# Attention plus routed MLP on one core: out-projection one block later, router search two blocks later, last key tiles moved forward

## Chip, cores and metric

The kernel runs on one core of a Trainium2 chip. The metric is the device time of one execution in microseconds. The engines named below are TensorE (PE, with its weight loads PEld), VectorE (DVE), ScalarE (ACT), GpSimd (POOL) and SyncE (SP), which issues nearly all DMAs.

## What is computed

The input x is one sequence of 2048 rows of 448 numbers. A layer norm, attention with 16 heads of 28 numbers over one shared key and one shared value head, an out-projection and a residual give h. A second layer norm of h feeds a router that picks 8 rows, and only those rows go through a gated MLP:

```python
x = A_x
h = x + _A_ref(_layernorm(x), A_wq, A_wk, A_wv, A_wo)
# _A_ref: q of 16 heads, one k, one v; softmax(q k^T * 28**-0.5) v; then @ wo
xn = _layernorm(h)
# _B_ref(xn): r = xn @ w_r; idx = the 8 largest r;
#   y = silu(xn[idx] @ w_gate) * (xn[idx] @ w_up) @ w_down * sigmoid(r[idx])
#   returns xn with y added at the rows idx
h2 = h + _B_ref(xn, B_w_r, B_w_gate, B_w_up, B_w_down)
```

All tensors are bf16. The result has 2048 x 448 numbers.

## The kernel before

**Blocks.** Attention is done in 16 blocks b = 4*qb + g: 512 query rows (qb) by 4 heads (g). A block runs over 16 key tiles of 128 keys. For a key tile, PE makes the scores of the 4 heads in two units of two PSUM banks (`qk`), an engine turns them into exponentials, and PE multiplies these with the values into the block's accumulator bank 6 or 7 (`act_pv`, `dve_pv`). Exponentials are made in two ways. On most tiles ACT makes them (line 753, one ACTIVATE of 128x1024 for a unit, PSUM banks 0 to 3 in turn); this text calls one such instruction "an exponential". On a few tiles of each block DVE approximates them: four TENSOR_SCALARs of 128x512 from PSUM banks 4 and 5 (line 766) and three shifts of 128x2048 (line 772) for a tile, which this text calls Y and shift. The list `groups` and the table `where` say which tiles of a block are DVE's: none in block 0, three in blocks 4, 8 and 12, four in the others, 57 in all. That leaves 199 tiles, or 398 exponentials, to ACT.

**The end of a block** (`post_block`). DVE copies the accumulator to `Ot` (line 551). Its row of softmax sums then goes through memory: SP stores it (`l_scr<-Ot`), loads it as 128x16 (`Lc<-l_scr`), DVE takes the reciprocal (line 560), SP stores that (`l_scr<-Lc`) and loads it broadcast over partitions (`Rb<-l_scr`). POOL multiplies `Ot` and `Rb` into `On` (line 563).

**Out-projection and second layer norm** (`out_proj`). When the four heads of a query block have their `On`, four steps k of 128 rows follow. PE multiplies `On` with `wo_pad` into one PSUM bank; DVE adds the residual into `hbuf` (line 579), takes the statistics (lines 581 and 582), POOL raises the variance to the power -0.5 (line 585, tile `st`), and DVE writes the normed row, the output row and the router's score (lines 587 to 601). This text calls these DVE instructions one LN chain. After k = 3, SP stores `out_dram<-x_sb` and `xn_scr<-xn`, 448 KB each. This happens for the first three query blocks; the last one has its own shorter path (`last_pre`, `last_proj`).

**Router.** After the third query block, `first_top` gathers 1536 scores: a matmul and a copy to `r12` (line 622) and three DMAs that lay them out in one row (`xnT<-r`); the second and third wait until the first has landed. `first_max` finds the 8 largest with MAX (line 628) and their places with MAX_INDEX (line 630), both on DVE. `second_top` uses the places to gather 8 rows by two indirect DMAs on POOL's queue. After the last block the remaining 512 scores are searched and the MLP of the 8 rows runs: the tail of the program.

**What sets the order.** The program's five instruction streams are made by `_Graph`. Each step is entered with a priority, its due time in key tiles: block b starts at 16*b. `plan` lists the steps with a duration and a latency for each (the number `lat` for a DMA, 2000 ns unless given), takes at each point the available step with the lowest priority, and so fixes the order on every engine. On the chip each engine runs its list strictly in that order, and waits on semaphores where data comes from another engine. `at(t, f, ...)` near line 803 gives out-projection, router and the rest their due times. `misc_bank` gives the PSUM bank that the Q projection, the out-projection and the router's matmul share: the one of banks 6 and 7 that the running block doesn't accumulate in.

Of the kernel before, what the change touches and what calls it, by code (L numbers as in the profile page):

```python
# [230 lines left out]
def _main(nc, G, sb, ps, psb, flag, scr, xs, A_x, A_wq, A_wk, A_wv, A_wo, B_w_r, B_w_gate, B_w_up, B_w_down, out,  # L231
# [4 lines left out]
    NT, NQB, CK, NB = S // 128, S // 512, 112, 16  # L236
# [58 lines left out]
    Rb = sb("Rb", [128, 2, 512], F32)  # L295
# [46 lines left out]
    def misc_bank(b):  # L342
        return 7 - b % 2
# [18 lines left out]
    def dma(o, i, writes, reads=(), prio=None, lat=2000.0):  # L362
        op = G.op(SP, lambda e: e.dma_start(o, i), 60, reads=reads, writes=writes, dma=True, prio=prio)
        op.lat = lat
        return op
# [6 lines left out]
    for i in range(4, NT, 4):  # L372
# [3 lines left out]
         reads=["idi"], writes=["ident"])  # L376
# [15 lines left out]
    for i in range(4):  # L392
        G.op(PO, lambda e, i=i: e.tensor_copy(wk_rep[0:CK, :, 32 * i:32 * i + DH], wk_sb[0:CK, :, :]), 300,
             reads=["wk_sb"], writes=["wk_rep"])
    G.op(PO, lambda e: e.memset(wq_pad[:, :, :, :], 0.0), 1800, writes=["wq_pad"])
    for ch in range(NCH):
        v = wq_pad[0:CK, ch, :, :].rearrange("p g (i c) -> p (g i) c", c=32)[:, :, 0:DH]
        G.op(PO, lambda e, ch=ch, v=v: e.tensor_copy(v, wq_sb[0:CK, ch, :].rearrange("p (h d) -> p h d", d=DH)), 590,
             reads=["wq_sb"], writes=["wq_pad"])
    G.op(PO, lambda e: e.memset(wv_pad[:, :, :], 0.0), 210, writes=["wv_pad"])  # L400
    G.op(PO, lambda e: e.tensor_copy(wv_pad[0:CK, :, 1:1 + DH], wv_sb[0:CK, :, :]), 280,
         reads=["wv_sb"], writes=["wv_pad"])
# [120 lines left out]
    def post_block(b):  # L523
        g, qb, rb = b % 4, b // 4, b % 2
# [3 lines left out]
        if last:  # L528
            G.prio = u - 30
            for h in range(2):  # L530
# [3 lines left out]
                     reads=[pk(acc_bank(b)), ("On", 1, 1)], writes=[("OtH", h)])  # L534
            for h in range(2):
# [6 lines left out]
                     reads=[("RbH", h)], writes=[("RbH", h)])  # L542
                for k in (2 * h, 2 * h + 1):
# [3 lines left out]
                         reads=[pk(acc_bank(b)), ("RbH", h)], writes=[("OnQ", k)])  # L547
            G.prio = u
            dma(scr[b, 0], Ot[0:128:32, rb, :], [("scr0", b)], reads=[("OtH", 0), ("OtH", 1)])
        else:  # L550
# [5 lines left out]
             reads=["Lmn", ("Lc", rb)], writes=["Lmn"])  # L556
        G.op(DV, lambda e: e.tensor_tensor(Lmx[:, :], Lmx[:, :], Lc[:, rb, :], ALU.max), 85,
             reads=["Lmx", ("Lc", rb)], writes=["Lmx"])
        if not last:
            G.op(DV, lambda e: e.reciprocal(Lc[:, rb, :], Lc[:, rb, :]), 200, reads=[("Lc", rb)], writes=[("Lc", rb)])  # L560
            dma(scr[b, 1].rearrange("i (r k) -> (i r) k", k=16), Lc[:, rb, :], [("scr1", b)], reads=[("Lc", rb)])
            dma(Rb[:, rb, :], scr[b, 1].unsqueeze(1).broadcast_to([4, 32, 512]), [("Rb", rb)], reads=[("scr1", b)])
            G.op(PO, lambda e: e.tensor_tensor(On[:, qb % 2, g, :], Ot[:, rb, :], Rb[:, rb, :], ALU.mult), 1270,  # L563
                 reads=[("Ot", rb), ("Rb", rb)], writes=[("On", qb % 2, g)])
        if exact and g == 3:
# [5 lines left out]
    def out_proj(qb, k):  # L571
        t = qb * 4 + k
        hr = t % 4
        bank = misc_bank(4 * qb + 4)
        for g2 in range(0, 4, 2):
            G.op(PE, [mm(ps[:, bank, 0:D], On[:, qb % 2, g, k * 128:(k + 1) * 128], wo_pad[:, g, 0:D], g == 0, g == 3)
                      for g in range(g2, g2 + 2)], 2 * 200,
# [2 lines left out]
             reads=[pk(bank), ("x", t)], writes=[("h", hr)])  # L580
# [27 lines left out]
                [("xs", qb)], reads=[("xn", i) for i in range(t - 3, t + 1)])  # L608

    def first_top():  # L610
        bank = misc_bank(13)
        if exact:
            second_top()
            return
        first_row(bank)
# [109 lines left out]
    evs = []  # L725
    groups = [4] * NB
    groups[0] = 0
    for b in range(4, NB, 4):
        groups[b] = 3
    where = {0: (), 1: (9,), 2: (5, 11), 3: (3, 7, 11), 4: (1, 5, 9, 13)}  # L730
    dve_tiles, act_tiles = [], []
    for b in range(NB):
        d = where[groups[b]]
        for j in range(NT):
            if j in d:
                dve_tiles.append((b, j, 16.0 * b + j - 0.5))
            else:
                act_tiles.append((b, j, 16.0 * (b + (j - sum(k < j for k in d)) / (NT - len(d)))))
# [3 lines left out]
    def at(t, fn, *a):  # L742
        events.append((t, lambda: fn(*a)))
# [51 lines left out]
    for n, e_ in enumerate(pv_list):  # L795
        b = e_[-2]
        at(e_[0], e_[1], *e_[2:], b not in done, n == max(k for k, q in enumerate(pv_list) if q[-2] == b))
        done[b] = e_[0]
    for b in range(NB):
        at(max(16 * b + 16.3, done[b] + 0.01), post_block, b)  # L800
        if b + 2 < NB:
            at(16 * b + 6.5, q_project, b + 2, misc_bank(b))
        if b % 4 == 3:
            for k in range(4):
                if b < NB - 1:
                    at(16 * b + 25.0 + k * 1.6, out_proj, b // 4, k)
                else:
                    at(16 * b + (14.6 if k < 3 else 17.0) + 0.1 * k, last_pre, k)
                    at(16 * b + 20.0 + k, last_proj, k)
    at(16 * 11 + 36.0, first_top)  # L810
    at(16 * 14 + 4.0, first_max)
    at(16 * 15 + 2.0, second_top)
    at(16 * 2 + 8.0, last_w)

    if exact:
# [214 lines left out]
```

## Time and profile before

| what | value |
|---|---|
| median of 3 runs | 444.52 us (441.43 to 445.93) |
| profiled execution | 442.73 us |
| its span, first to last instruction | 441.3 us |
| busy: ACT, DVE, PE, POOL | 382.1, 366.5, 357.1, 46.8 us |
| mean granted TensorE clock | 0.944 of full speed |

The profile page counts only execution as busy. "Idle before" is the time that an engine stood before an instruction, with what released it. In a timeline, instructions of one kind that follow each other are merged, with their count behind x. DVE's durations overlap a little: two Y in a row show 1.28 us, and the next instruction starts 1.19 to 1.20 us after the first. So sums over DVE go by starts.

### The profile page before, as it was taken

Reading aid. Unit: us, or ns where it says so; the run is one execution under the profiler, and the core shown is the slowest. Engines: PE = TensorE matmul, PEld = TensorE weight load, DVE = VectorE, ACT = ScalarE, POOL = GpSimd, SP = SyncE. Lnnn points to the kernel's source line nnn. Section 1 sums busy time; section 2 is a strip of 40 time slices with the busy share of each in tenths; the row PEclk is TensorE's granted clock in tenths of the full one; section 3 lists DMA queues with packets and bytes.
Section 4 is the critical chain, followed back from the end, with each engine's and each line's share of the span. In section 5 each row is a group of like instructions: output and inputs, shape, how many; then the busy total and the mean of one; then the engine's idle time right before and its main releaser. Section 6 shows DMA issues by size and latency. Waiting matters only on the chain.

```text
span 441.3 us, 7932 instructions
## 1 busy us (share of the span) xinstructions
PE 357.1 (81%) x3243; PEld 106.7 (24%) x3243; DVE 366.5 (83%) x792; ACT 382.1 (87%) x425; POOL 46.8 (11%) x76
## 2 busy tenths in 40 slices
PE   0888898888887988989887988888879879887754
PEld 0333212222222222222221222222222212221243
DVE  4999629989788899899986898999988899995371
ACT  1397689999998999999996999999989998996640
POOL 8210001010101101010102110101011010111000
PEclk9998769999999999999998999999999998998955
DMA  8960000000000030000000030000000200000010
GB/s 227 272 186 11 0 1 27 4 26 1 26 3 25 1 94 17 22 8 26 1 24 4 3 108 3 26 3 25 4 25 1 88 24 4 25 7 22 1 43 8
DMA packets 17350, 15.75 MB, mean 36 GB/s; under 512 B 5944, under 2 KB 14428, under 8 KB 17308
## 3 DMA queue, kind: packets, MB, share of 16 engines
q1 hardware_dynamic: 17212, 15.16, 11.8%
q8 instruction: 27, 0.44, 0.4%
q14 instruction: 15, 0.12, 0.1%
q0 software_dynamic: 96, 0.02, 0.0%
HBM read 11.70 MB, written 3.47 MB: 34 GB/s over the span
## 4 chain that ended last, share of the span: by engine, by line
DVE 31%; ACT 29%; PE 25%; DMA 9%; POOL 2%; issue 1%; SPq 1%; POOLq 0%; DVEq 0%
ACT P L753 29%; PE ps L349 25%; DVE Y L766 11%; DVE Y L772 8%; DMA Rb<-l_scr 5%; DVE Ot L551 2%; DMA xnT<-r 2%; POOL On L563 1%; DMA x_sb<-in_A_x_dram 1%; DMA l_scr<-Lc 1%; DVE xn L479 1%; DVE bn L464 1%; DVE K L505 1%; DVE xnT L493 1%; DVE Vs L516 1%
## 5 line engine op out<-in xcount | busy, mean ns | idle before, releaser
L753 ACT ACTIVATE P<-ps 128x1024 bf16<-128x1024 f32 x398 | 370.7, 1082 | 26.3 <-PE ps L349 25.0
L349 PE MATMUL ps<-Q,K 64*128 64x512 bf16 x1024 | 187.0, 394 | 44.0 <-ACT P L753 26.6
L766 DVE TENSOR_SCALAR Y<-ps 128x512 int16<-128x512 f32 x228 | 146.8, 680 | 24.9 <-PE ps L349 24.5
L772 DVE TENSOR_SCALAR Y<-Y 128x2048 int16<-128x2048 int16 x171 | 117.7, 724 | 1.5
L349 PEld LDWEIGHTS ps<-Q,K 64*128 64x128 bf16 x1024 | 44.6, 93 | 191.7 <-ACT P L753 141.4
L349 PE MATMUL ps<-P,Vs 128*32 128x512 bf16 x796 | 81.2, 399 | 0.3 <-ACT P L753 0.3
L349 PE MATMUL ps<-Y,Vs 128*32 128x512 bf16 x912 | 75.2, 387 | 0.5 <-DVE Y L772 0.3
L563 POOL TENSOR_TENSOR On<-Ot,Rb 128x512 bf16<-128x512 f32 x15 | 21.7, 1446 | 280.8 <-DMA Rb<-l_scr 280.8
L349 PEld LDWEIGHTS ps<-P,Vs 128*32 128x32 bf16 x796 | 20.6, 93 | 51.7 <-issue 50.4
L349 PEld LDWEIGHTS ps<-Y,Vs 128*32 128x32 bf16 x912 | 22.7, 96 | 22.8 <-issue 11.5
L349 PE MATMUL ps<-xnT,wq_pad 112*128 112x512 bf16 x64 | 21.8, 437 | 4.0 <-DVE Ot L551 3.5
L349 PE MATMUL ps<-wo_pad,On 128*128 128x448 bf16 (+1 forms) x64 | 18.0, 378 | 8.5 <-POOL On L563 7.7
L551 DVE COPY Ot<-ps 128x512 f32<-128x512 f32 x15 | 10.3, 688 | 8.0 <-PE ps L349 7.6
L456 DVE TENSOR_SCALAR Q<-ps,qone 128x512 bf16<-128x512 f32 x16 | 11.7, 730 | 5.9 <-PE ps L349 5.8
L352 PE MATMUL ps<-ident,xn 128*112 128x128 bf16 x64 | 6.3, 259 | 11.2 <-POOL vone L405 10.6
L464 DVE BATCH_NORM_STATS2 bn<-x_sb 128x6 f32<-128x448 bf16 x16 | 9.3, 602 | 4.4 <-DMA x_sb<-in_A_x_dram 4.4
L585 POOL TENSOR_TENSOR st<-st,nhalf 128x1 f32<-128x1 f32 x12 | 7.7, 641 | 48.1 <-DVE st L583 48.1
L579 DVE TENSOR_TENSOR hbuf<-ps,x_sb 128x448 f32<-128x448 f32 x12 | 7.4, 619 | 4.6 <-PE ps L349 4.5
L349 PEld LDWEIGHTS ps<-wo_pad,On 128*128 128x128 bf16 x64 | 4.7, 100 | 17.7 <-POOL On L563 8.8
L352 PEld LDWEIGHTS ps<-ident,xn 128*112 128x112 bf16 x64 | 5.2, 161 | 13.3 <-POOL vone L405 10.6
L598 DVE SCALAR_TENSOR_TENSOR junk<-hbuf,st,w_rb 128x448 bf16<-128x448 f32 x12 | 8.1, 677 | 0.0
L349 PEld LDWEIGHTS ps<-xnT,wq_pad 112*128 112x128 bf16 x64 | 4.4, 104 | 14.7 <-DVE Ot L551 7.0
(164 smaller groups left out, 158.8 us busy)
## 6 DMA issues: line engine op xcount, KB each, us to landing
Rb<-l_scr SPq DMA_DIRECT2D x15, 256.0 KB
wg_sb<-in_B_w_gate_dram SPq DMA_DIRECT2D x1, 1568.0 KB, 12.0
wu_sb<-in_B_w_up_dram SPq DMA_DIRECT2D x1, 1568.0 KB, 17.6
wd_sb<-in_B_w_down_dram SPq DMA_DIRECT2D x1, 1568.0 KB, 21.1
x_sb<-in_A_x_dram SPq DMA_DIRECT2D x3, 448.0 KB, 6.4
out_dram<-x_sb SPq DMA_DIRECT2D x3, 448.0 KB, 2.9
xn_scr<-xn SPq DMA_DIRECT2D x3, 448.0 KB, 3.9
x_sb<-in_A_x_dram SPq DMA_DIRECT2D x2, 224.0 KB, 2.9
```

What stands on the lines that cost most here:

```text
L349: return lambda e: e.matmul(o, lhsT=l, rhs=r, start=start, stop=stop)
L352: return lambda e: e.transpose(o, i, ident[0:p, 0:p])
L456: G.op(DV, lambda e: e.tensor_scalar(Q[:, b % 4, :], ps[:, bank, :], qone[:, 0:1], None, ALU.add), dvt(512), reads=[pk(bank), "qone"], wri ...
L464: G.op(DV, [lambda e, t=t: e.bn_stats(bn6[:, t, :], x_sb[:, t, 0:D])], dvt(D), reads=[("x", t)], writes=[("bn6", t)])
L551: G.op(DV, lambda e: e.tensor_copy(Ot[:, rb, :], ps[:, acc_bank(b), :]), dvt(512), reads=[pk(acc_bank(b))], writes=[("Ot", rb)], prio=u - 30)
L563: G.op(PO, lambda e: e.tensor_tensor(On[:, qb % 2, g, :], Ot[:, rb, :], Rb[:, rb, :], ALU.mult), 1270, reads=[("Ot", rb), ("Rb", rb)], wri ...
L579: G.op(DV, lambda e: e.tensor_tensor(hbuf[:, hr, :], ps[:, bank, 0:D], x_sb[:, t, 0:D], ALU.add), dvt(D), reads=[pk(bank), ("x", t)], writ ...
L585: G.op(PO, lambda e: e.tensor_tensor(st[:, t, 4:5], st[:, t, 7:8], nhalf[:, 0:1], ALU.pow), 570, reads=[("st7", t), "nhalf"], writes=[("st ...
L598: G.op(DV, lambda e: e.scalar_tensor_tensor(junk[:, :], hbuf[:, hr, :], st[:, t, 4:5], w_rb[:, :], ALU.mult, ALU.mult, accum_out=st[:, t, ...
L753: G.op(AC, lambda e: e.activation(P[:, sl, :, :], ps[:, b0:b0 + 2, :], ACT.Exp, bias=EBIAS, scale=OCT), 905, reads=[pk(b0), pk(b0 + 1)], w ...
L766: G.op(DV, lambda e, k=k: e.tensor_scalar(Y[:, n, 0, p + 2 * k, :].bitcast(I16), ps[:, 4 + k, :], 0.0, 32639.0 - 3 * STEP, ALU.max, ALU.mi ...
L772: G.op(DV, lambda e: e.tensor_scalar(Y[:, n, v, :, :].bitcast(I16), Y[:, n, 0, :, :].bitcast(I16), v * STEP, None, ALU.add), 610, reads=[( ...
```

## The change

Six edits, all in due times, tables and the planner's latencies; no operation is added, removed or resized.

- The out-projection of query block qb is due from 12.5 key tiles later (37.5 instead of 25.0 after the start of the query block's last block), and its four steps lie 2.0 instead of 1.6 apart. So it falls into the second block after, not the first. Its PSUM bank changes with that block from 7 to 6.
- The blocks with three DVE tiles follow: 5, 9 and 13 instead of 4, 8 and 12.
- The planner counts 4800 instead of 2000 ns for the load of `Rb`.
- The router's first search is due later: `first_top` 229 instead of 212, `first_max` 233 instead of 228, `second_top` 245 instead of 242, with the bank that fits.
- In the last block DVE's tiles are 0, 3, 7 and 10 instead of 1, 5, 9 and 13.

```diff
-            dma(Rb[:, rb, :], scr[b, 1].unsqueeze(1).broadcast_to([4, 32, 512]), [("Rb", rb)], reads=[("scr1", b)])
+            dma(Rb[:, rb, :], scr[b, 1].unsqueeze(1).broadcast_to([4, 32, 512]), [("Rb", rb)], reads=[("scr1", b)], lat=4800.0)
...
     def out_proj(qb, k):
-        bank = misc_bank(4 * qb + 4)
+        bank = misc_bank(4 * qb + 5)
...
     def first_top():
-        bank = misc_bank(13)
+        bank = misc_bank(14)
...
-    for b in range(4, NB, 4):
+    for b in range(5, NB, 4):
         groups[b] = 3
...
-        d = where[groups[b]]
+        d = where[groups[b]] if b < NB - 1 else (0, 3, 7, 10)
...
-                    at(16 * b + 25.0 + k * 1.6, out_proj, b // 4, k)
+                    at(16 * b + 37.5 + k * 2.0, out_proj, b // 4, k)
...
-    at(16 * 11 + 36.0, first_top)
-    at(16 * 14 + 4.0, first_max)
-    at(16 * 15 + 2.0, second_top)
+    at(16 * 14 + 5.0, first_top)
+    at(16 * 14 + 9.0, first_max)
+    at(16 * 15 + 5.0, second_top)
```

**PE, the first out-projection.** Before, in block 4; `Q,K` are scores, `P,Vs` and `Y,Vs` the products with the values, `wo_pad,On` the out-projection, `xnT,wq_pad` a Q projection:

```order
L349 MATMUL ps<-Y,Vs 32x512 x8
L349 MATMUL ps<-Q,K 128x512 x2
L349 MATMUL ps<-wo_pad,On 128x448 x4
L349 MATMUL ps<-Q,K 128x512 x2
L349 MATMUL ps<-P,Vs 32x512 x4
L349 MATMUL ps<-Q,K 128x512 x2
L349 MATMUL ps<-Y,Vs 32x512 x8
L349 MATMUL ps<-wo_pad,On 128x448 x2
```

PE after the change, in block 5:

```order
L349 MATMUL ps<-P,Vs 32x512 x4
L349 MATMUL ps<-Q,K 128x512 x2
L349 MATMUL ps<-wo_pad,On 128x448 x2
L349 MATMUL ps<-Q,K 128x512 x2
L349 MATMUL ps<-P,Vs 32x512 x4
L349 MATMUL ps<-Q,K 128x512 x2
L349 MATMUL ps<-wo_pad,On 128x448 x2
L349 MATMUL ps<-Q,K 128x512 x4
L349 MATMUL ps<-P,Vs 32x512 x4
L349 MATMUL ps<-xnT,wq_pad 128x512 x2
```

Counted in the exponentials whose scores PE makes between the wait for the `Ot` copy of the query block's last block and the first `wo_pad,On`, there were 12 in each of the three stages; now there are 22, 24 and 24. The four matmuls of a step are now split in twos with scores between, and the Q projection, in the same bank, stands between steps 0 and 1.

**POOL, the first two stages.** Before (`st` is the power of the LN chain, `On` the multiplication of a block's end):

```order
L563 TENSOR_TENSOR On<-Ot,Rb 128x512 x4
L585 TENSOR_TENSOR st<-st,nhalf 128x1 x4
L563 TENSOR_TENSOR On<-Ot,Rb 128x512 x4
L585 TENSOR_TENSOR st<-st,nhalf 128x1 x4
L563 TENSOR_TENSOR On<-Ot,Rb 128x512 x4
```

POOL after the change:

```order
L563 TENSOR_TENSOR On<-Ot,Rb 128x512 x4
L585 TENSOR_TENSOR st<-st,nhalf 128x1
L563 TENSOR_TENSOR On<-Ot,Rb 128x512
L585 TENSOR_TENSOR st<-st,nhalf 128x1 x3
L563 TENSOR_TENSOR On<-Ot,Rb 128x512 x3
```

The multiplication of the block that has just ended (4, 8, 12) now stands between the first and the second power of the LN chains.

**SP and DVE, the router's first search.** SP before, from the load of block 12's `Rb` on (the stores `out_dram` and `xn_scr` belong to the third out-projection, the next `l_scr<-Ot` to block 13):

```order
L363 DMA out_dram<-x_sb 128x4x448
L363 DMA xn_scr<-xn 128x4x448
L363 DMA Rb<-l_scr 128x1x512
L363 DMA xnT<-r 1x4x128 x3
L363 DMA l_scr<-Ot 4x512
```

SP after the change:

```order
L363 DMA Rb<-l_scr 128x1x512
L363 DMA out_dram<-x_sb 128x4x448
L363 DMA xn_scr<-xn 128x4x448
L363 DMA l_scr<-Ot 4x512
L363 DMA xnT<-r 1x4x128
L363 DMA Lc<-l_scr 128x16
L363 DMA xnT<-r 1x4x128 x2
```

DVE before, from the copy to `r12` to the end of the search in block 13:

```order
L622 COPY r<-ps 12x128
L772 TENSOR_SCALAR Y<-Y 128x2048
L456 TENSOR_SCALAR Q<-ps,qone 128x512
L766 TENSOR_SCALAR Y<-ps 128x512 x2
L772 TENSOR_SCALAR Y<-Y 128x2048 x2
L766 TENSOR_SCALAR Y<-ps 128x512 x2
L772 TENSOR_SCALAR Y<-Y 128x2048
L628 MAX top<-xnT 1x8
L766 TENSOR_SCALAR Y<-ps 128x512 x2
L630 MAX_INDEX idx<-top,xnT 1x8
```

DVE after the change, in block 14, from the `Ot` copy of block 13 on:

```order
L551 COPY Ot<-ps 128x512
L772 TENSOR_SCALAR Y<-Y 128x2048
L766 TENSOR_SCALAR Y<-ps 128x512 x2
L622 COPY r<-ps 12x128
L772 TENSOR_SCALAR Y<-Y 128x2048 x3
L766 TENSOR_SCALAR Y<-ps 128x512
L555 TENSOR_TENSOR Lmn<-Lmn,Lc 128x16
L557 TENSOR_TENSOR Lmx<-Lmx,Lc 128x16
L560 RECIPROCAL Lc<-Lc 128x16
L766 TENSOR_SCALAR Y<-ps 128x512
L628 MAX top<-xnT 1x8
```

The search moved behind the copy of block 13, with five shifts and Y and block 13's reciprocal between `r12` and MAX instead of eight shifts and Y and a Q copy, and the layout DMAs are now shared out among those of block 13's end.

**PE, the last block.** Before, around the first matmuls of `last_pre`, which wait for the `On` of block 14:

```order
L349 MATMUL ps<-Q,K 128x512 x6
L349 MATMUL ps<-P,Vs 32x512 x4
L349 MATMUL ps<-Q,K 128x512 x2
L349 MATMUL ps<-wo_pad,On 128x450 x2
L349 MATMUL ps<-Q,K 128x512 x2
L349 MATMUL ps<-P,Vs 32x512 x4
L349 MATMUL ps<-Y,Vs 32x512 x4
```

PE after the change:

```order
L349 MATMUL ps<-Q,K 128x512 x4
L349 MATMUL ps<-P,Vs 32x512 x4
L349 MATMUL ps<-Y,Vs 32x512 x4
L349 MATMUL ps<-wo_pad,On 128x450 x2
L349 MATMUL ps<-Q,K 128x512 x2
L349 MATMUL ps<-Y,Vs 32x512 x4
```

Between the wait for block 14's `Ot` and this first `wo_pad,On` PE made the scores of 12 exponentials; now it makes those of 15, with 6 left until the end instead of 9.

## Rows read from the trace of the kernel before

**Rows 1.** The page's groups: line, engine, tiles, count | busy, mean ns | idle before

```profile
L753 ACT ACTIVATE P<-ps 128x1024 bf16<-128x1024 f32 x398 | 370.7, 1082 | 26.3 <-PE ps L349 25.0
L766 DVE TENSOR_SCALAR Y<-ps 128x512 int16<-128x512 f32 x228 | 146.8, 680 | 24.9 <-PE ps L349 24.5
L772 DVE TENSOR_SCALAR Y<-Y 128x2048 int16<-128x2048 int16 x171 | 117.7, 724 | 1.5
```

**Rows 2.** ACT's timeline from block 3 on: start, us, what, [idle before]

```profile
142.51 91.32 ACT L753 ACTIVATE P<-ps 128x1024 bf16<-128x1024 f32 x98 [1.65 <-PE ps L349]
237.04 2.11 ACT L753 ACTIVATE P<-ps 128x1024 bf16<-128x1024 f32 x2 [3.21 <-PE ps L349]
239.47 89.42 ACT L753 ACTIVATE P<-ps 128x1024 bf16<-128x1024 f32 x96 [0.33 <-PE ps L349]
330.54 31.56 ACT L753 ACTIVATE P<-ps 128x1024 bf16<-128x1024 f32 x34 [1.65 <-PE ps L349]
362.76 2.85 ACT L753 ACTIVATE P<-ps 128x1024 bf16<-128x1024 f32 x3 [0.66 <-PE ps L349]
366.66 1.94 ACT L753 ACTIVATE P<-ps 128x1024 bf16<-128x1024 f32 x2 [1.04 <-PE ps L349]
368.75 32.22 ACT L753 ACTIVATE P<-ps 128x1024 bf16<-128x1024 f32 x35 [0.16 <-PE ps L349]
403.45 1.02 ACT L753 ACTIVATE P<-ps 128x1024 bf16<-128x1024 f32 x1 [2.48 <-PE ps L349]
404.96 1.02 ACT L753 ACTIVATE P<-ps 128x1024 bf16<-128x1024 f32 x1 [0.49 <-PE ps L349]
406.52 6.88 ACT L753 ACTIVATE P<-ps 128x1024 bf16<-128x1024 f32 x7 [0.53 <-PE ps L349]
```

**Rows 3.** Chain of waits, end of block 3 to the first out-projection: start, us, what

```profile
128.00 0.70 DVE Ot L551
...
130.91 0.75 DVE Q L456
...
132.85 0.08 DVE Lmn L555
...
133.21 1.41 DMA l_scr<-Lc
...
134.63 5.13 DMA Rb<-l_scr
...
139.84 1.33 POOL On L563
...
141.21 3.28 PE ps L349 x24
```

**Rows 4.** Busy time by engine while ACT runs without a gap

```profile
142.50:233.80 91.30, 79.23 (x718) 21.42 (x714) 84.62 (x169) 90.92 (x98) 7.26 (x8) 1.00 0.08 24
```

**Rows 5.** DVE's and POOL's timeline: shifts, and the first LN chain

```profile
133.10 1.83 DVE L772 TENSOR_SCALAR Y<-Y 128x2048 int16<-128x2048 int16 x3
...
138.74 2.97 DVE L772 TENSOR_SCALAR Y<-Y 128x2048 int16<-128x2048 int16 x3
...
142.18 0.62 DVE L579 TENSOR_TENSOR hbuf<-ps,x_sb 128x448 f32<-128x448 f32 x1 [0.48 <-PE ps L349]
...
143.72 0.15 DVE L583 TENSOR_SCALAR st<-mv 128x1 f32<-128x1 f32 x1
...
144.54 0.15 DVE L587 TENSOR_SCALAR st<-st 128x1 f32<-128x1 f32 x1 [0.66 <-POOL st L585]
...
146.26 0.62 DVE L579 TENSOR_TENSOR hbuf<-ps,x_sb 128x448 f32<-128x448 f32 x1
```

**Rows 6.** Chain of waits, the router's first search

```profile
350.36 0.19 DVE r L622
...
350.57 5.75 DMA xnT<-r
...
356.96 1.63 DMA xnT<-r
...
358.68 1.75 DVE top L628
360.43 1.19 DVE Y L766 x2
361.62 1.74 DVE idx L630
```

**Rows 7.** Timeline, end of block 14 to the last block's wait

```profile
388.12 0.69 DVE L551 COPY Ot<-ps 128x512 f32<-128x512 f32 x1 [0.15 <-PE ps L349]
...
400.26 1.62 POOL L563 TENSOR_TENSOR On<-Ot,Rb 128x512 bf16<-128x512 f32 x1 [7.42 <-DMA Rb<-l_scr]
401.93 0.93 PE L349 MATMUL ps<-wo_pad,On 128*128 128x450 bf16 x2 [2.35 <-POOL On L563]
```

**Rows 8.** Longest waits: engine, line, waited for, us in total, times, longest

```profile
PE ps L349 <- DVE Y L766: 8.1, 18, 1.1
```

## Prediction

> **What bounds the kernel now.** I read the page's groups first. ACT is busy longest: 398 exponentials with 370.7 us, and the 26.3 us idle before them were nearly all ended by PE [rows 1]. So I took ACT's timeline next. From 142.51 us on it shows runs without a gap (98 exponentials in 91.32 us, one each 0.932 us) and a few stops [rows 2]. Such a run is a stretch in which ACT alone sets the time; a stop is time that a better order can give back. The stops before 142 us lie in the first blocks, whose order stays as it is up to the end of block 3. Those behind it fall into three kinds:
>
> - 1.65, 3.21 + 0.33 and 1.65 us, together 6.84 us, at 141, 234 and 329 us, one for each out-projection;
> - 0.66 + 1.04 + 0.16 = 1.86 us at 362 to 369 us, beside the router's search;
> - 2.48 + 0.49 + 0.53 = 3.50 us at 401 to 407 us, in the last block.
>
> The reader is to see their cause in the chain of waits. At the first out-projection the copy of `Ot` starts at 128.00; the load of `Rb` alone takes 5.13 us; the multiplication ends at 141.17, 13.2 us after the copy began, and PE starts at 141.21 [rows 3]. PE got there after 12 exponentials, 12 x 0.932 = 11.2 us, and stood at the head of its queue with the next scores behind it: ACT ran dry. In the last block it is the same: copy at 388.12, multiplication done at 401.88, 13.8 us later, PE idle 2.35 us [rows 7]. At the router DVE is late: it waits for the layout DMAs, and then MAX and MAX_INDEX hold it for 1.75 and 1.74 us [rows 6]; PE waits for DVE's Y, and ACT for PE. DVE has little room: while ACT ran gap-free it was busy 84.62 of 91.30 us [rows 4].
>
> **The out-projection, its latency for Rb and the three-tile blocks.** PE now reaches the first out-projection after 22, 24 and 24 exponentials, so at the earliest 22 x 0.932 = 20.5 us after the copy, against 13.2 us for the chain. The wait goes, with 7 us to spare: 6.84 us. What is late next? The LN chains fall into one block with three tiles. By starts, DVE has there: the copy 0.70, a Q copy 0.75, the three small ones before the reciprocal's store 0.25 (132.85 to 133.10), ten Y at 0.60 and seven shifts at 0.61 (1.83 for three), and four LN chains. One chain is 143.72 - 142.18 = 1.54 up to the power and 146.26 - 144.54 = 1.72 behind it, 3.3 us with the last small step [rows 3, 5, 6]. Sum: 0.70 + 0.75 + 0.25 + 6.0 + 4.3 + 13.2 = 25.2 us. ACT has 28 exponentials there, 26.1 us. It fits, with 0.9 us left; in the first stage, with nine Y and five shifts, with more.
>
> The new wait is on POOL. The power of step 1 now stands behind the multiplication of the block just ended, which waits for its `Rb`. It can end no sooner than 13.2 us after that block's copy, the power some 0.6 us later. Behind the power on DVE stand the rest of chain 1 and then Y. DVE gets there about 13.5 us after the copy: step 2's matmul, whose sum it does first, stands 12 exponentials (11.2 us) behind the copy, plus 0.9 us for scores and matmul, plus half a chain of 1.5 us. So DVE stands some 0.3 us, covered by the 0.9 us left. The nearest measured wait for a power is 0.66 us [rows 5]; three of these, 2.0 us, is the upper end, zero the lower. I take 0.3 us in all.
>
> **The router's search.** The 1.86 us go with block 13's order, but the search now lies between the copies of blocks 13 and 14. ACT has 22 exponentials there, 20.5 us. DVE has the copy 0.70, fourteen Y 8.4, eleven shifts 6.7, the small ones 0.25, `r12` 0.19, MAX and MAX_INDEX 3.5 [rows 6] and two casts, about 20 us. Block 13's multiplication on POOL lies beside it: three shifts beside such a one took 2.97 instead of 1.83 us [rows 5], so 1.1 more. Then MAX's wait. `r12` stands 2.7 us behind the copy (0.70 + 0.61 + 1.2 + 0.2). The first layout DMA took 5.75 us when it was queued behind two stores of 448 KB and the load of `Rb`; the last landed 1.63 us after its issue [rows 6]. Now `Rb` is issued before the stores, and the stores are some 3.4 us old when `r12` is ready (a shift and the last score lie before the copy, 0.7 us, then the 2.7), so I take 2.0 us, near the lower row. The second and third add 0.6 + 1.63 us. That is 7.0 us behind the copy; DVE is there at 6.0. Sum for DVE: 20 + 1.1 + 1.0 = 22.1, against 20.5 us. Of the 1.6 us ACT's double buffer hides some 0.5: I take 1.0 us lost. With 1.63 us and no contention nothing is lost; with 5.75 us the wait is 4.7 and the loss 5 us.
>
> The row shows 1.1 us lost beside a multiplication of 1.33 us [rows 3, 5]. The Trainium skill (SBUF — State Buffer, section "SBUF: two separate sides") says that such a shift and a POOL instruction hold one port pair exclusively, so that the loser is fully blocked. By that rule each such meeting costs up to the whole 1.3 us; with one here and one in the last block the sum would be 0.4 us longer, 434.5.
>
> **The last block.** PE reaches the matmuls that wait for block 14's `On` after 15 instead of 12 exponentials, 14.0 us after the copy, against 13.8 us: the 2.48 us go, and the two stops after it, which came while PE was catching up. DVE's last tile comes three key tiles earlier, so from the copy to its last shift DVE has 12 Y, 11 shifts, the copy and some small ones, 15.3 us, 16.4 beside the multiplication, against 17 exponentials, 15.8 us. I take 0.5 us lost; the bounds are 0 and, if PE waits as before, 3.5. The tail behind the last exponential keeps its instructions: nothing.
>
> **The sum.** Given back: 6.84 + 1.86 + 3.50 = 12.2 us. Lost: 0.3 + 1.0 + 0.5 = 1.8. Net 10.4 us: 442.73 of the profiled execution becomes 432.3. The median of the runs lies 1.8 us above that execution, so I forecast 434.0 us. Its own range, with the lost terms from 0 to twice what I took and the chain's spread, is 431 to 437.
>
> **Rivals.**
> - The layout DMAs stay slow. They are still issued behind the two stores, and the trace has 5.75 us for that; for it speaks that the stores are issued right before block 13's copy. DVE loses 5 instead of 1 us, and the last block, which has no room, can't make it up: 438.3 us. Against: the load of `Rb` no longer stands between.
> - DVE becomes the bound. The stops were also DVE's time to catch up. At the page's means (0.68 for Y, 0.724 for a shift, which include contention), four blocks with their LN chains cost 60 x 0.68 + 45 x 0.724 + 4 x 1.7 + 13.2 = 93.4 us, against 98 x 0.932 = 91.3 for ACT: 2.1 us lost in each of three periods. Net 10.4 - 6.3 = 4.1, so 440.3 us, no change that shows. Against: by starts DVE had 7% idle in the gap-free run [rows 4].
> - Slower: the shared bank. Out-projection steps and the Q projection now take turns in bank 6, and PE, in order, must wait five times in a stage for DVE to empty it, 15 times in all, with ACT's scores queued behind. If each wait were as long as PE's longest for a Y, 1.1 us [rows 8], that costs 16.5 us: 450.5 us, 1.4% slower than before. It decides from 0.7 us each, where the gain of 10.4 is used up. Against: in the order two to four exponentials lie between emptying and refilling, and no wait of PE for `hbuf` shows before.
>
> **How the numbers follow.** I give the forecast 0.62, the slow layout DMAs 0.18, DVE as bound 0.11 and the bank 0.09. A measurement of this kernel tells about 1% from no change, so faster means under 440.1 us: the first two, 0.80. Within 1%: 0.11. Slower by over 1%: 0.09. The range reaches from 430 (nothing lost) over the forecast and the slow DMAs to 440.5, which leaves most of the last rival and part of the third outside.
>
> **What would show it.** Right: no stop of ACT at an out-projection, the `Rb` wait of PE gone from the waits, MAX waiting about 1 us, ACT's last exponential some 10 us earlier, the tail as long as before. Wrong: new rows of PE waiting for `hbuf` or Q, DVE waiting for the power by 1 us or more, MAX waiting 4 us, or a stop at the last block's first out-projection matmul.

## The result, and the profile after

| what | before | after |
|---|---|---|
| median | 443.07 us (4 runs, 441.43 to 445.93) | 429.19 us (4 runs, 427.93 to 430.99) |
| profiled execution, its span | 442.73, 441.3 us | 429.03, 427.6 us |
| busy: ACT, DVE, PE, POOL | 382.1, 366.5, 357.1, 46.8 us | 380.6, 363.0, 353.3, 50.6 us |
| granted TensorE clock | 0.944 | 0.958 |

After over before is 0.9683 (95% interval 0.9614 to 0.9752): faster. I had forecast 434.0 us, with a range of 430.0 to 440.5; the result lies 0.8 us below the range. The direction and the mechanism were right, the size was not.

ACT's timeline answers to [rows 2]: start, us, what, [idle before].

```profile
102.28 297.56 ACT L753 ACTIVATE P<-ps 128x1024 bf16<-128x1024 f32 x321 [0.40 <-PE ps L349]
402.05 0.38 ACT L539 ACTIVATE Rb<-ps 128x256 f32<-128x256 f32 x1 [2.22 <-PE ps L349]
```

From 102.28 on, 321 exponentials follow each other in one run. Before, the same 321 stood between 102.09 and 413.40, with ten stops among them, the idle times in [rows 2]. Ahead of the runs shown there stand the first 42:

```profile
102.09 38.77 ACT L753 ACTIVATE P<-ps 128x1024 bf16<-128x1024 f32 x42 [0.35 <-PE ps L349]
```

The last one now ends at 399.84 instead of 413.40, 13.56 us earlier. What follows it takes as long as before: 427.6 - 399.84 = 27.8 us against 441.3 - 413.40 = 27.9. So the whole gain lies where the stops were.

The profile page's groups, as in [rows 1]:

```profile
L753 ACT ACTIVATE P<-ps 128x1024 bf16<-128x1024 f32 x398 | 369.3, 1107 | 14.2 <-PE ps L349 12.8
...
L766 DVE TENSOR_SCALAR Y<-ps 128x512 int16<-128x512 f32 x228 | 147.4, 682 | 18.0 <-PE ps L349 18.0
L772 DVE TENSOR_SCALAR Y<-Y 128x2048 int16<-128x2048 int16 x171 | 116.0, 710 | 1.4
```

ACT's idle time fell by 12.1 us, and DVE's Y and shifts are as long as before. Now the losses that I had expected. DVE's waits in the stretch 102.3 to 399.8 (waited for: us in total, times, longest), and DVE's and POOL's timeline around the last out-projection and the router:

```profile
DVE Y L766 <- PE ps L349: 12.8, 23, 1.1
DVE Q L456 <- PE ps L349: 4.9, 6, 1.2
DVE hbuf L579 <- PE ps L349: 2.5, 4, 1.6
DVE top L628 <- DMA xnT<-r: 0.5, 1, 0.5
```

```profile
344.05 1.27 POOL L563 TENSOR_TENSOR On<-Ot,Rb 128x512 bf16<-128x512 f32 x1 [4.53 <-DMA Rb<-l_scr]
345.29 0.54 POOL L585 TENSOR_TENSOR st<-st,nhalf 128x1 f32<-128x1 f32 x1
...
363.47 1.75 DVE L628 MAX8 top<-xnT 1x8 f32<-1x1536 f32 x1 [0.52 <-DMA xnT<-r]
...
368.92 3.50 POOL L563 TENSOR_TENSOR On<-Ot,Rb 128x512 bf16<-128x512 f32 x1 [15.50 <-DMA Rb<-l_scr]
369.40 1.87 DVE L772 TENSOR_SCALAR Y<-Y 128x2048 int16<-128x2048 int16 x3
```

The power does stand right behind the multiplication, as foreseen (345.29 behind 344.05 + 1.27), but no wait of DVE for it shows. MAX waits 0.52 us (0.65 before, with the slow layout DMAs of [rows 6]); ACT doesn't stop. DVE still waits 12.8 us for PE before a Y: it has room.

Busy time by engine between the copies that bound blocks 5, 9 and 13 (columns: us, PE, PEld, DVE, ACT, POOL, clock, DMA share, GB/s). These are the blocks that now hold the LN chains:

```profile
150.20:174.80 24.60, 22.23 (x184) 5.94 (x184) 22.25 (x63) 24.41 (x28) 4.60 (x5) 1.00 0.05 14
241.01:265.67 24.66, 22.36 (x186) 5.94 (x184) 23.97 (x67) 24.42 (x28) 4.59 (x5) 1.00 0.05 14
331.88:356.53 24.65, 22.35 (x186) 5.94 (x184) 23.97 (x67) 24.42 (x28) 4.59 (x5) 1.00 0.05 14
```

I had worked out 25.2 us of DVE in such a block; it was busy 22.25 to 23.97. In the last block, where PE stood 2.35 us [rows 7], POOL's multiplication ended at 391.94 and PE came at 393.13 without a wait:

```profile
390.16 1.78 POOL L563 TENSOR_TENSOR On<-Ot,Rb 128x512 bf16<-128x512 f32 x1 [3.84 <-DMA Rb<-l_scr]
...
393.13 0.56 PE L349 MATMUL ps<-wo_pad,On 128*128 128x450 bf16 x2
```

### The profile page after: what moved, and what is told of

Same layout as the page of the kernel before. It is cut to its first block, busy times and chain, and to the rows that moved or that the text cites. A ratio compares the mean times of both kernels' runs of the same rounds, so it can differ in the third digit from the quotient of the medians.

```text
span 427.6 us, 7935 instructions
## 1 busy us (share of the span) xinstructions
PE 353.3 (83%) x3243; PEld 106.0 (25%) x3243; DVE 363.0 (85%) x792; ACT 380.6 (89%) x425; POOL 50.6 (12%) x76
## 3 DMA queue, kind: packets, MB, share of 16 engines
q1 hardware_dynamic: 17212, 15.16, 12.1%
## 4 chain that ended last, share of the span: by engine, by line
ACT 56%; PE 22%; DVE 18%; DMA 1%; issue 1%; SPq 1%; POOL 0%; POOLq 0%; DVEq 0%
ACT P L753 55%; PE ps L349 22%; DVE Y L766 5%; DVE Y L772 4%; DMA x_sb<-in_A_x_dram 1%; DVE xn L479 1%; DVE Ot L551 1%; DVE bn L464 1%; DVE K L505 1%; DVE xnT L493 1%; DVE Vs L516 1%; SPq L363 1%; DVE bn L687 1%; DVE junk L656 1%; DVE junk L664 0%
## 5 line engine op out<-in xcount | busy, mean ns | idle before, releaser
L753 ACT ACTIVATE P<-ps 128x1024 bf16<-128x1024 f32 x398 | 369.3, 1107 | 14.2 <-PE ps L349 12.8
L772 DVE TENSOR_SCALAR Y<-Y 128x2048 int16<-128x2048 int16 x171 | 116.0, 710 | 1.4
L349 PE MATMUL ps<-Y,Vs 128*32 128x512 bf16 x912 | 74.3, 383 | 0.0
L349 PEld LDWEIGHTS ps<-P,Vs 128*32 128x32 bf16 x796 | 20.5, 93 | 49.3 <-issue 48.3
L585 POOL TENSOR_TENSOR st<-st,nhalf 128x1 f32<-128x1 f32 x12 | 10.1, 841 | 65.8 <-DVE st L583 65.8
L352 PE MATMUL ps<-ident,xn 128*112 128x128 bf16 x64 | 6.3, 259 | 11.2 <-POOL vone L405 10.5
L352 PEld LDWEIGHTS ps<-ident,xn 128*112 128x112 bf16 x64 | 5.2, 161 | 13.3 <-POOL vone L405 10.5
L581 DVE BATCH_NORM_STATS2 bn<-hbuf 128x6 f32<-128x448 f32 x12 | 7.5, 622 | 0.1
```

The costliest lines, as they stand in the source:

```text
L349: return lambda e: e.matmul(o, lhsT=l, rhs=r, start=start, stop=stop)
L352: return lambda e: e.transpose(o, i, ident[0:p, 0:p])
L585: G.op(PO, lambda e: e.tensor_tensor(st[:, t, 4:5], st[:, t, 7:8], nhalf[:, 0:1], ALU.pow), 570, reads=[("st7", t), "nhalf"], writes=[("st ...
L753: G.op(AC, lambda e: e.activation(P[:, sl, :, :], ps[:, b0:b0 + 2, :], ACT.Exp, bias=EBIAS, scale=OCT), 905, reads=[pk(b0), pk(b0 + 1)], w ...
L772: G.op(DV, lambda e: e.tensor_scalar(Y[:, n, v, :, :].bitcast(I16), Y[:, n, 0, :, :].bitcast(I16), v * STEP, None, ALU.add), 610, reads=[( ...
```

## Experiments

Four questions: which edit removes which stop; whether a stop costs more than its idle time; whether DVE has room; and whether the whole change is needed. The experiments form three groups: one edit at a time; the distance in between with the room on DVE; side by side. The kernel before ran beside each group, and kernels of different groups are compared by their ratio to it: 442.26 us (19 runs) in the first, 443.73 (7) in the second, 441.11 (11) in the third.

### One edit at a time

**Out-projection alone.**

```diff
-        bank = misc_bank(4 * qb + 4)
+        bank = misc_bank(4 * qb + 5)
...
-    for b in range(4, NB, 4):
+    for b in range(5, NB, 4):
...
-                    at(16 * b + 25.0 + k * 1.6, out_proj, b // 4, k)
+                    at(16 * b + 37.5 + k * 2.0, out_proj, b // 4, k)
...
-    at(16 * 11 + 36.0, first_top)
+    at(16 * 11 + 45.0, first_top)
```

> The kernel before with only the out-projection's edits: due time one block later, its bank, the three-tile blocks at 5, 9 and 13. The router's first matmul must come behind the third out-projection, so its due time goes from 212 to 221, no further. Theory (each stop of ScalarE has its own cause, and costs its idle time plus about 0.1 us for the restart, and VectorE has room): the three stops of 1.65, 3.54 and 1.65 us at the out-projections go, the stops at the router and in the last block stay; 443.07 - 6.84 - 0.4 = 435.8 us. Rival (VectorE was held together by these stops and is late where the LN chains now stand): new waits of PE for Y, 438 us or more. Rival (one edit carries the whole gain, and it is this one): 430 us.

Measured: 431.71 us, ratio 0.9776 (0.9706 to 0.9846). ACT's timeline:

```profile
99.51 289.16 ACT L753 ACTIVATE P<-ps 128x1024 bf16<-128x1024 f32 x312 [0.34 <-PE ps L349]
391.00 2.12 ACT L753 ACTIVATE P<-ps 128x1024 bf16<-128x1024 f32 x2 [2.33 <-PE ps L349]
393.95 6.93 ACT L753 ACTIVATE P<-ps 128x1024 bf16<-128x1024 f32 x7 [0.83 <-PE ps L349]
```

The median is 10.5 us below that of the kernel before, where 7.2 were expected. The three stops went, and those at the router with them, 1.86 us that the theory had left standing; whether the little move of `first_top` or the new order around it removed them, this run does not tell. Only the last block's stops are left. PE's waits for Y (line 766) came to 2.1 us, against 6.0 in the kernel before over the same 100 to 400 us, so the rival of a late DVE falls here.

**The latency alone.**

```diff
-            dma(Rb[:, rb, :], scr[b, 1].unsqueeze(1).broadcast_to([4, 32, 512]), [("Rb", rb)], reads=[("scr1", b)])
+            dma(Rb[:, rb, :], scr[b, 1].unsqueeze(1).broadcast_to([4, 32, 512]), [("Rb", rb)], reads=[("scr1", b)], lat=4800.0)
```

> The kernel before with only the planner's latency for Rb at 4800. The order then has the three out-projections two exponentials later than before (14 instead of 12 behind the copy of Ot) and the last block's first out-projection matmul four later. Theory: each out-projection stop shrinks by about 2 x 0.93 = 1.86 us, so 1.65, 1.86 and 1.65, and the last block's 3.50 us go: 8.7 us with the restarts, 434.4 us, with about 1.7 us left at the second out-projection and the router's 1.9 us. Rival (the due time of the out-projection is what counts, the latency moves little): 439.5 us, only the last block's 3.5 us gone.

Measured: 427.86 us, ratio 0.9655 (0.9588 to 0.9722), 6.5 us better than expected and no slower than the whole change. ACT's timeline, then POOL's and PE's:

```profile
102.02 255.96 ACT L753 ACTIVATE P<-ps 128x1024 bf16<-128x1024 f32 x277 [0.40 <-PE ps L349]
358.29 40.88 ACT L753 ACTIVATE P<-ps 128x1024 bf16<-128x1024 f32 x44 [0.31 <-PE ps L349]
```

```profile
139.67 1.43 POOL L563 TENSOR_TENSOR On<-Ot,Rb 128x512 bf16<-128x512 f32 x1 [19.84 <-DMA Rb<-l_scr]
...
141.55 0.55 PE L349 MATMUL ps<-wo_pad,On 128*128 128x448 bf16 x2
```

At the first out-projection the multiplication ends at 141.10, 13.17 us after the copy (127.93), and PE comes at 141.55, 13.62 us after it. Before, PE was free 11.64 us after the copy [rows 3]: at 139.64, since it stood 1.57 us until 141.21. Two exponentials more of distance, 14 instead of 12, were enough; the move by a whole block was not needed. Nine of the ten stops are gone, and 0.31 us is left near the router.

Why the router's stops shrank, with its own edit not made, is in DVE's timeline. The first two rows are of the kernel before, the last two of the latency alone:

```profile
352.39 0.75 DVE L456 TENSOR_SCALAR Q<-ps,qone 128x512 bf16<-128x512 f32 x1 [1.25 <-PE ps L349]
...
358.68 1.75 DVE L628 MAX8 top<-xnT 1x8 f32<-1x1536 f32 x1 [0.65 <-DMA xnT<-r]
```

```profile
345.25 0.75 DVE L456 TENSOR_SCALAR Q<-ps,qone 128x512 bf16<-128x512 f32 x1
...
351.13 1.75 DVE L628 MAX8 top<-xnT 1x8 f32<-1x1536 f32 x1 [1.27 <-DMA xnT<-r]
```

The latency changed the order here too: three shifts and a Y now stand between `r12` and the Q copy, where one shift stood, and DVE no longer waits for PE there. MAX waits longer than before, but the two waits together fell from 1.90 to 1.27 us.

**The router alone.**

```diff
-        bank = misc_bank(13)
+        bank = misc_bank(14)
...
-    at(16 * 11 + 36.0, first_top)
-    at(16 * 14 + 4.0, first_max)
-    at(16 * 15 + 2.0, second_top)
+    at(16 * 14 + 5.0, first_top)
+    at(16 * 14 + 9.0, first_max)
+    at(16 * 15 + 5.0, second_top)
```

> The kernel before with only the router's edit (first search about 16 exponentials later, other bank). Theory: 1.86 us and a restart go, all else stays: 441.0 us; MAX waits for its layout DMAs by less than 1 us, since they are no longer queued right behind the two stores and the load of Rb. Rival (the prediction's lost terms exist, and were hidden in the whole change by the room that the other edits made): with the stores still early, MAX waits 1 us and three shifts beside POOL's multiplication take 2.97 us again, nothing is gained, 443 us.

Measured: 440.48 us, ratio 0.9931 (0.989 to 0.9973). The router's stops went and MAX waited for nothing. In the profiled execution the third out-projection's stop grew from 1.65 us to 2.53 + 0.50. PE stood 1.57 us there, as before; but the granted clock then was 0.50 from 328.5 to 331.5 us, and the four matmuls behind the stand took 1.59 instead of 0.94 us. The next section comes back to this.

**The last block's tiles alone.**

```diff
-        d = where[groups[b]]
+        d = where[groups[b]] if b < NB - 1 else (0, 3, 7, 10)
```

> The kernel before with only VectorE's tiles of the last block moved forward (0, 3, 7, 10 instead of 1, 5, 9, 13). The first out-projection matmul of the last block stays where it was in PE's order. Theory: the stop at that matmul (2.48 us) stays, since POOL's multiplication ends no sooner; the two small ones behind it (0.49 and 0.53 us), at which PE waited for VectorE's late tile, go: 442.0 us. Rival (the tiles were what made the last block stop): 439.4 us. Rival (VectorE, with four tiles in ten, falls behind): a new wait for Y in the last block, 444 us.

Measured: 440.66 us, ratio 0.9963 (0.9925 to 1.0): no change that shows. The stop stayed at 2.65 us, and, against my expectation, so did the small ones behind it (0.49, 0.93 and 0.33 us). So DVE's late tile is not their cause. They come while PE catches up behind the stop, with the granted clock at 0.50 from 402 to 407 us; with the latency alone, and the tile still late, they went with the stop.

### The distance in between

The latency again, with 3600 instead of 4800.

```diff
-            dma(..., [("Rb", rb)], reads=[("scr1", b)])
+            dma(..., [("Rb", rb)], reads=[("scr1", b)], lat=3600.0)
```

> The kernel before with the planner's latency for Rb at 3600: the three out-projections stand one exponential later in PE's order than before (13 behind the copy of Ot; before 12, with 4800 it was 14), the last block's first matmul two later. Theory A (a stop is as long as PE comes too early, each by itself): each out-projection stop shrinks by 0.93 us, 1.65, 3.54, 1.65 to 0.72, 2.6, 0.72; the last block's 2.48 to 0.6; the router's 1.9 stays; 442.3 less 5 to 6 us, 436.5 us. Theory B (a stop also holds VectorE up, and its work then piles up, so that the longer second stop and the stops at the router were consequences of the first ones): with shorter stops those go altogether, and about 0.7 us is left at each out-projection: 431.5 us.

Measured: 432.43 us, ratio 0.9745 (0.9675 to 0.9814). ACT's timeline, as in [rows 2]:

```profile
141.88 90.77 ACT L753 ACTIVATE P<-ps 128x1024 bf16<-128x1024 f32 x98 [0.36 <-PE ps L349]
233.00 90.77 ACT L753 ACTIVATE P<-ps 128x1024 bf16<-128x1024 f32 x98 [0.35 <-PE ps L349]
324.13 30.76 ACT L753 ACTIVATE P<-ps 128x1024 bf16<-128x1024 f32 x33 [0.36 <-PE ps L349]
355.72 2.85 ACT L753 ACTIVATE P<-ps 128x1024 bf16<-128x1024 f32 x3 [0.83 <-PE ps L349]
359.62 36.08 ACT L753 ACTIVATE P<-ps 128x1024 bf16<-128x1024 f32 x39 [1.05 <-PE ps L349]
396.14 6.88 ACT L753 ACTIVATE P<-ps 128x1024 bf16<-128x1024 f32 x7 [0.44 <-PE ps L349]
```

The time is near theory B's; its reason is not borne out. One exponential more of distance took the second out-projection's stop from 3.54 to 0.35 us, far more than its own 0.93. But the router's two stops stayed, as theory A had it, and with them DVE's two waits, 1.22 us at the Q copy and 0.67 at MAX. What made the second stop long is in PE's timeline: first and second out-projection of the kernel before, then the second with 3600.

```profile
141.21 0.94 PE L349 MATMUL ps<-wo_pad,On 128*128 128x448 bf16 x4 [1.57 <-POOL On L563]
...
234.78 1.67 PE L349 MATMUL ps<-wo_pad,On 128*128 128x448 bf16 x4 [2.17 <-POOL On L563]
236.39 0.61 PE L349 MATMUL ps<-Q,K 64*128 64x512 bf16 x2
```

```profile
232.09 0.55 PE L349 MATMUL ps<-wo_pad,On 128*128 128x448 bf16 x2 [0.28 <-POOL On L563]
232.57 0.39 PE L349 MATMUL ps<-Q,K 64*128 64x512 bf16 x2
```

Before, PE stood 2.17 us at the second, 0.6 longer than at the first: it came as early (11.60 us after the copy), but the chain took 13.72 us, mostly since POOL's multiplication took 1.76 instead of 1.32. The four matmuls behind the stand took 1.67 instead of 0.94 us, the next scores 0.61 instead of 0.39. The granted clock (the last but two column) shows why. The first row is the block around that out-projection in the kernel before, the second the same block with the latency of 4800:

```profile
221.01:248.94 27.93, 23.18 (x184) 6.13 (x182) 21.48 (x52) 24.21 (x27) 3.39 (x4) 0.94 0.04 11
```

```profile
218.36:242.78 24.42, 22.42 (x190) 6.25 (x188) 23.16 (x53) 24.29 (x28) 2.98 (x3) 1.00 0.04 13
```

Inside the block the clock of the kernel before fell to 0.50 of full speed, the level of 1.2 GHz, and so it did at the router and in the last block; the changed kernel has 1.00, the level of 2.4 GHz, over its whole run of exponentials.

```profile
235.00:237.00 2.00, 2.00 (x10) 0.48 (x8) 0.51 (x1) 0.00 (x0) 0.00 (x0) 0.50 0.00 0
364.50:367.50 3.00, 2.90 (x22) 0.61 (x26) 3.00 (x6) 1.96 (x3) 0.00 (x0) 0.50 0.02 5
402.00:405.00 3.00, 3.00 (x16) 0.43 (x16) 0.00 (x0) 1.06 (x2) 0.00 (x0) 0.50 0.00 0
```

The length of the stand alone does not decide whether the clock falls. With the last block's tiles alone PE stood 1.57 us at the first and at the second out-projection; behind the first the four matmuls took 0.93 us, behind the second 1.68, and the clock there was 0.50:

```profile
140.83 0.93 PE L349 MATMUL ps<-wo_pad,On 128*128 128x448 bf16 x4 [1.57 <-POOL On L563]
...
233.88 1.68 PE L349 MATMUL ps<-wo_pad,On 128*128 128x448 bf16 x4 [1.57 <-POOL On L563]
```

Behind a stand of 1.57 us ACT stopped for 1.65 us where the clock held, and for 2.94 to 3.03 us in the three places where it fell (two with the router's edit alone, one with the tiles alone). So a fall costs about 1.3 us, and the 3.54 us of the kernel before are 1.65 + 0.6 + 1.3. Why the clock falls in one place and holds in another is left open. With 3600 PE stands 0.28 us there and the clock holds; and only two of these matmuls stand ahead of the next scores, not four.

### Room on DVE

Three kernels with six exponentials fewer: three of ACT's key tiles go to DVE. The first gives the changed kernel five DVE tiles in blocks 3, 7 and 11; the second gives the kernel with the latency alone five in blocks 2, 6 and 10; the third gives the changed kernel four, not three, in the blocks with the LN chains.

```diff
+    for b in (3, 7, 11):
+        groups[b] = 5
-    where = {0: (), 1: (9,), 2: (5, 11), 3: (3, 7, 11), 4: (1, 5, 9, 13)}
+    where = {0: (), 1: (9,), 2: (5, 11), 3: (3, 7, 11), 4: (1, 5, 9, 13), 5: (1, 4, 7, 10, 13)}
```

> The changed kernel with five instead of four of VectorE's key tiles in blocks 3, 7 and 11: six exponentials fewer on ScalarE (392 instead of 398), three tiles more on VectorE (3 x 4.2 us). Theory (VectorE has room, about 10% of the stage): ScalarE stays without a stop and ends 6 x 0.927 = 5.6 us earlier, 423.6 us. Rival (VectorE was at its limit, as the prediction took it with 1.8 us of lost terms): PE waits for Y in these blocks, the gain is eaten, 429 us or more.

Measured: 427.72 us, ratio 0.9612 (0.9526 to 0.9699). Some of the 5.6 us came through, but ACT got nine stops from 178 us on, the longest 1.69 and 1.82 us.

```diff
+    for b in (2, 6, 10):
+        groups[b] = 5
-    where = {0: (), 1: (9,), 2: (5, 11), 3: (3, 7, 11), 4: (1, 5, 9, 13)}
+    where = {0: (), 1: (9,), 2: (5, 11), 3: (3, 7, 11), 4: (1, 5, 9, 13), 5: (1, 4, 7, 10, 13)}
```

> The kernel before with the latency of 4800 and, beside it, five of VectorE's key tiles in blocks 2, 6 and 10. Theory (room on VectorE): 427.9 - 5.6 = 422.3 us. Rival (no room): 428 us or more, with PE waiting for Y in the blocks of five.

Measured: 425.27 us, ratio 0.9577 (0.951 to 0.9644). Between theory and rival; ACT's longest stops were 1.37 and 1.63 us.

```diff
-        groups[b] = 3
+        groups[b] = 4
```

> The changed kernel with four of VectorE's key tiles also in the blocks with the LN chains (5, 9, 13): six exponentials fewer, and three tiles more on VectorE just where it has most to do. By the prediction's sum VectorE needs 25.2 us in such a block with three tiles, so 29.4 us with four, while ScalarE's exponentials there (26 x 0.93) take 24.1 us. Theory (what counts is the room inside the block, since the scores of VectorE's tiles have one pair of banks): about 4 us of stops in each, 12 us against 5.6 us saved, 435 us. Rival (the room of the whole stage counts, a block's backlog is worked off later): 423.6 us.

Measured: 435.91 us, ratio 0.9812 (0.9741 to 0.9883): the theory's 435. Busy time in blocks 5, 9 and 13, to be laid beside the three rows of the changed kernel above:

```profile
150.93:177.65 26.72, 24.29 (x204) 6.69 (x202) 24.04 (x66) 25.41 (x29) 3.42 (x5) 1.00 0.12 40
242.64:271.10 28.46, 25.16 (x204) 6.28 (x202) 26.67 (x69) 24.92 (x27) 4.43 (x5) 0.94 0.14 44
335.64:363.62 27.98, 24.34 (x204) 6.14 (x202) 27.57 (x73) 25.50 (x28) 3.45 (x5) 1.00 0.11 34
```

DVE was busy 27.57 of 27.98 us in block 13, and the blocks took 26.72, 28.46 and 27.98 instead of 24.60, 24.66 and 24.65 us: 2.1, 3.8 and 3.3 us more, where the theory had 4 each. In block 9 the granted clock fell as well (0.94), and block 14 stopped ACT for another 2.17 + 0.65 + 0.33 us, which the theory did not have, so the sum came out better than its parts. Still, the changed kernel's LN blocks lie within one tile of DVE's limit, and room elsewhere in the stage didn't help: what counts here is the block.

### Side by side

The changed kernel, the latency alone and two placements of five tiles, on one chip. The last one's edit against the third's:

```diff
-    for b in (2, 6, 10):
+    for b in (3, 7, 11):
```

> The changed kernel as it is, beside the next three on one chip. Theory (nothing but the latency's two exponentials of distance is needed, the other edits neither give nor cost much): 428.5 us, within 1% of the next. Rival (the other edits cost VectorE or POOL something, as the multiplication of 3.50 us on POOL suggests): over 1% slower than the next.

> The kernel before with only the latency of 4800, again, to be compared with the changed kernel on one chip. Theory: 427.9 us as before, within 1% of the changed kernel. Rival (its 14 exponentials are on the edge, and in some executions PE comes too early for the multiplication): a spread of several us, or a median above the changed kernel's.

> The latency of 4800 and five of VectorE's tiles in blocks 2, 6 and 10, again. Theory: 2.6 us (0.6%) faster than the latency alone, so of the six exponentials' 5.6 us about half comes through, since VectorE was busy 23.82 of 23.89 us in block 10 and ScalarE got new stops of 1.37, 0.31, 0.40, 0.54 and 1.63 us. Rival (the difference between the two calls was chance): the same as the latency alone.

> The same with the five tiles in blocks 3, 7 and 11, where VectorE was busy less with the latency alone (18.48 of 21.79 us in block 3, 20.18 of 22.48 in block 11, against 21.30 of 22.08 in block 10). Theory (room inside the block counts): fewer and shorter stops than with 2, 6 and 10, about 3.5 of the 5.6 us come through, 424 us. Rival (the LN chains follow in the next block, and VectorE enters them late): stops in blocks 4, 8 and 12, 427 us or more.

| kernel | median, us | ratio to before |
|---|---|---|
| the changed kernel | 428.78 | 0.9704 (0.9655 to 0.9754) |
| latency alone | 428.07 | 0.9697 (0.9651 to 0.9744) |
| latency, five tiles in 2, 6, 10 | 426.68 | 0.9646 (0.9598 to 0.9694) |
| latency, five tiles in 3, 7, 11 | 437.18 | 0.9892 (0.9847 to 0.9937) |

The changed kernel and the latency alone can't be told apart. Five tiles in blocks 2, 6 and 10 were ahead of the latency alone in both groups, by the ratios 0.8 and 0.5%; side by side that is 1.4 us, and the intervals overlap both times. In blocks 3, 7 and 11, which had more idle time on DVE, the same three tiles made the kernel 9 us slower than the latency alone. The time is the rival's: the LN chains stand in blocks 4, 8 and 12 there. The changed kernel, whose chains stand one block further, took five tiles in 3, 7 and 11 without such a loss (427.72 us, ratio 0.9612), which speaks for the rival too. That the chains came late is argued, not shown.

The latency alone also tested a term of my forecast. Its profile has these two rows, of ACT and of DVE:

```profile
99.53 296.98 ACT L753 ACTIVATE P<-ps 128x1024 bf16<-128x1024 f32 x321 [0.40 <-PE ps L349]
...
348.47 1.75 DVE L628 MAX8 top<-xnT 1x8 f32<-1x1536 f32 x1 [1.07 <-DMA xnT<-r]
```

MAX held DVE up for 1.07 us, and ACT ran all 321 exponentials without a stop. In the first profile of the same kernel it was 1.27 us, and ACT stopped for 0.31 us.

## Why the prediction was right, and where it was wrong

**Right: what bounds the kernel, and what the change gives back.** ACT's stops came from PE standing at the head of its queue for `On`, and all 12.2 us of them went, at the places named. The tail stayed. None of the three rivals came: MAX waited 0.52 us, not 4.7; PE waited for a Y 6 times in the stretch, 1.7 us in all, 0.5 at most (before, in its own stretch, 12 times, 4.9 us, 1.0 at most); no wait of PE for `hbuf` or Q in bank 6 appeared.

**Wrong: the step "Lost: 0.3 + 1.0 + 0.5 = 1.8".** ACT ran without a stop, so all three terms measured zero. Each took a time for which DVE is held up and passed it on to ACT, less at most 0.5 us for ACT's double buffer, a number that came from no row. The runs show that DVE's delay reaches ACT only when the block's room is used up. A wait of 1.07 us at MAX cost nothing, one of 1.27 us no more than 0.31; one tile more in the LN blocks, 4.2 us, made these 2.1 to 3.8 us longer. For an LN block I had the room nearly right, though both figures were too long: 25.2 us of DVE in 26.1, where DVE was busy 22.25 to 23.97 us and the block lasted 24.60 to 24.66, so 0.7 to 2.4 us were left where I had 0.9. The 0.3 us for the power I charged although my own sum covered it. For the block with the search I had no room, 22.1 us against 20.5 of ACT. DVE was busy 20.21 us there, near the 20 without wait and contention, and the block had 21.83 us, all of them ACT's:

```profile
356.53:378.36 21.83, 18.14 (x175) 4.82 (x175) 20.21 (x36) 21.83 (x25) 3.50 (x1) 1.00 0.18 56
```

The 1.1 us of contention did not fall on DVE: the three shifts beside the multiplication took 1.87 us (2.97 in [rows 5]), and POOL's multiplication 3.50. The rule that I had weighed there (the Trainium skill, SBUF — State Buffer, section "SBUF: two separate sides": of two instructions that need the shared ports the one that starts second is fully blocked) would have made the sum 0.4 us longer. The trace agrees that one of the two was held up; but it was POOL, whose span began 0.48 us before the first shift and ended 1.15 us behind the last one, and nothing on the path waited for it. Spans on POOL are rough, so which of them really started first is open.

**Wrong: the size of a stop.** I counted a stop at its idle time. The 321 exponentials and their stops were 13.75 us shorter (311.31 to 297.56), 1.55 us more than the 12.2 us of stops. ACT's busy time in the stretch fell by that:

```profile
102.10:413.40 311.30, 266.60 (x2381) 72.07 (x2374) 272.81 (x539) 298.07 (x321) 28.56 (x27) 0.98 0.07 22
```

```profile
102.30:399.80 297.50, 262.82 (x2381) 71.29 (x2374) 268.28 (x539) 296.52 (x321) 32.53 (x27) 1.00 0.07 23
```

The first is before, the second after. An exponential alone takes 1.02 us, each further one in a run adds 0.92 (1.94 for two, [rows 2]): ten stops fewer are 1.0 us. The other 0.5 us is pace inside the runs, which I can't place.

**Wrong: "The median of the runs lies 1.8 us above that execution".** This was added as if it belonged to the kernel. It was the chance of three runs: with more, before's medians were 443.07, 442.26, 443.73 and 441.11 us, around the 442.73 of the profiled execution. After's median lies 0.2 us above its own.

Together: 1.8 + 1.5 + 1.6 = 4.9, against 434.0 - 429.2 = 4.8 us. The lower end of the range, 430, stood for nothing lost (442.7 - 12.2 = 430.5); it left out what a stop costs beyond its idle time, and with that the same sum gives 429.0.

**Right for another reason.** I put the out-projection's 6.84 us down to its due time, the router's 1.86 to its own edit and only the last block's 3.50 to the latency. The sum holds for the whole change, but the latency alone takes nearly all of it. At the router the reading was incomplete: besides MAX, DVE waited 1.25 us at the Q copy, and the stop of 1.04 us came with the granted clock at 0.50, where four score matmuls took 1.03 us (0.60 with the latency alone). The step "with 7 us to spare" should have been a question: how much spare is enough? PE came 11.64 us after the copy to a chain of 13.2; two exponentials, 1.86 us, closed that gap.

## What to carry over

Where an in-order engine stands for a chain of known length, the fix is to tell the planner that length; here one number (2000 to 4800 ns for a load that took 5.13 us) gave as much as the whole change. In these runs a wait on the engine that feeds the bounding one cost nothing until the room of its block was used up, so such terms belong in the range, with zero as the likely value, and not in the sum. By the placements tried here, more work for that engine goes where no other burst follows in the next block; the idle time of the block itself was not enough to choose by.

## What I had not expected of the hardware

A stand of PE of the same length, 1.57 us, was followed by a granted clock of 0.50 in three places and left it at 1.00 in others, within one execution too; a stop of ACT was 1.3 us longer where it fell.

Two executions of one kernel can part in the first 100 us. The stretch 30 to 60 us in the two profiles of the latency alone:

```profile
30.00:60.00 30.00, 24.77 (x184) 8.18 (x182) 22.11 (x47) 23.07 (x25) 1.01 (x1) 0.78 0.04 11
```

```profile
30.00:60.00 30.00, 23.55 (x188) 8.77 (x188) 21.89 (x45) 23.15 (x26) 1.01 (x1) 0.89 0.04 11
```

The granted clock there was 0.78 and 0.89 of full speed. In the second the 321 exponentials began at 99.53 instead of 102.02 us, and the execution took 425.54 instead of 428.40 us: the start makes up 2.5 of the 2.9 us. They ran on two chips, but the out-projection alone, on the chip of the first, began its run at 99.51 us too, with 0.94 in that stretch.
